# Dividing the softmax by its sum after the product with the values, with the reciprocals spread by two transposes a block

## The chip, the cores and the metric

One NeuronCore of a Trainium2 chip. The metric is the device time of one execution in microseconds (us). Engines are named as in the profile: PE (TensorE), PEld (its weight load), DVE (VectorE), ACT (ScalarE), POOL (GpSimd), SP (the queue that issues DMAs).

## What is computed

For 4 images of 8 heads (768 rows, 64 columns a head) the reference hashes q and k with 6 projections, lets a row see only the keys with its own hash, and takes an exact softmax:

```python
scores = scale * np.matmul(q, k.transpose(0, 1, 3, 2))
scores = np.where(mask, scores, -1000000000.0)
scores = scores - np.max(scores, axis=-1, keepdims=True)
attn = np.exp(scores)
attn = attn / (np.sum(attn, axis=-1, keepdims=True) + 1e-09)
return np.matmul(attn, v).astype(np.float32)
```

The heads laid side by side (512 columns) then go through a gated feed-forward stage: `h = relu(x @ w_in)`, a 3-tap convolution along the rows, `h * sigmoid(conv) @ w_out`, 1024 hidden columns. The weights and taps arrive as 64-bit floats.

## The kernel before, in words

The four images are worked one after the other. An image has four pairs of heads; a pair has three **blocks** of 256 query rows; a block has four **units** (2 heads x 2 tiles of 128 rows). So there are 192 units and 48 blocks. `Pair.prepare` (L202 on) splits q and k of the next pair into high and low parts on POOL (L167, L172) and has SP copy them into place (L170, L174), and hashes on PE (L182); the hash bits pass DVE (L185) and POOL (L187).

A unit passes these steps:

- `products` (L249, PE): scores s, 4 matmuls into PSUM ring S, which has three slots for s, the transposes t and the hash;
- `maximum` (DVE): L257 copies s to SBUF tile e and takes the row maximum; `total` (L264) adds 1e-9 to the sum of the unit before; L261 scales the maximum;
- `exponential` (L267, ACT): exp, with the row sum gathered into column 2 of the small tile st;
- `normalise`, one unit later: reciprocal of the sum (L272, DVE), then e times it (L273, POOL, 128x768);
- `transposes` (L278, PE), LAG = 3 units later: six 128x128 transposes of e into ring S; `to_sbuf` (L285, ACT) copies them to at.

After the transposes of a block's last unit its `values` are listed: 6 chunks x 2 heads on PE (L298, 24 matmul instructions, here "the v group") into half of a 512-column PSUM tile of ring M (two slots). They run in one go in the next iteration of four (AVS = (6, 0, 0, 0)), behind that iteration's transposes. An iteration later ACT copies the result to xh (L303), and one more later DVE puts the rest in xl (L306): x is kept as a high and a low part. For the last block of an image the values run inside the feed-forward stage (`fill`, L461), after its first `hidden`.

The loop (L408 on) writes out the order of each engine by hand; engines run in order and wait for one another by semaphores. In an iteration come: products, maximum, transposes and copy of unit i-3, exp, normalise of unit i-1, xl, the v group, a step of `prepare`, then `background`. `background` (L125) runs the decoding of weights from 64-bit floats: 16 blocks of 128x512, each with five DVE steps (L87, L89, L91, L93, L95), ACT casts (L85, L103) and two POOL steps (L105, L107), one block begun every 3.6 iterations. It lasts through the first image and into its feed-forward stage. `ffn` (L367) has hidden matmuls (L323), activation and taps (L328 to L342) and the output matmuls (L353).

Of the kernel before, what the change touches and what calls it, by code (L numbers as in the profile page):

```python
# [7 lines left out]
F32 = mybir.dt.float32  # L8
# [4 lines left out]
ALU = mybir.AluOpType  # L13

B, H, S, D = 4, 8, 768, 64
NB = 6
DM, DFF = 512, 1024
P = 128
NP = H // 2
NCK = S // P  # L20
HS = S // 2
QB = 256
# [6 lines left out]
F64_MIN = 2.0 ** -15 * 1.125  # L29
LAG, EB = 3, 5  # L30
FLAG = 3
AVS = (6, 0, 0, 0)
PREP = (3, 2, 1)
PREP_N = 6
W0 = 6
# [6 lines left out]
def lsh_attention_conv_ffn(ctx, tc, qk, v, hw, w_in, conv_w, w_out, consts, ident_in, out):  # L42
    nc = tc.nc
    PSUM = bass.MemoryType.PSUM
    cp = ctx.enter_context(tc.tile_pool(name="const", bufs=1))
    wp = ctx.enter_context(tc.tile_pool(name="work", bufs=1))
# [4 lines left out]
    def ring(pool, bufs, shape, dtype, tag, name):  # L51

        k = turns[tag] = (turns.get(tag, -1) + 1) % bufs
        return pool.tile(shape, dtype, tag=f"{tag}{k}", name=name, bufs=1)


    ident = cp.tile([P, P], F32, name="ident")
# [51 lines left out]
    def decode_taps(raw):  # L109
        up, low = yield from decode(raw, NFC * 3, "cw")  # L110
        nc.vector.tensor_tensor(cw.rearrange("p f k -> p (f k)"), up, low, ALU.add)
# [7 lines left out]
    def fetch(n):  # L119

        for src, name in blocks[:n]:
            raw = cp.tile([P, 2 * WC], I32, tag=f"w{name}", name=f"raw{name}")
            nc.sync.dma_start(raw, src)
            fetched.append((raw, name))
        del blocks[:n]  # L125
# [111 lines left out]
    class Unit:  # L237
# [11 lines left out]
                    nc.tensor.matmul(self.sp[:, half, :HS], A[:, h, qs], C[:, h, half * HS:(half + 1) * HS],  # L249
                                     start=(kk == 0), stop=(kk == 1))  # L250

        def maximum(self, prev):

            self.st = ring(wp, 8, [P, 4], F32, "st", f"st{self.nm}")
            e = wp.tile([P, 776], F32, tag="e", name=f"e{self.nm}", bufs=EB)
            self.e = e[:, :S]
            nc.vector.tensor_scalar(self.e.rearrange("p (a b) -> p a b", a=2), self.sp[:, :, :HS],  # L257
                                    MASKED, None, ALU.max, ALU.max, accum_out=self.st[:, 0:1])
            if prev:
                prev.total()  # L260
            nc.vector.tensor_scalar(self.st[:, 1:2], self.st[:, 0:1], -SCALE, None, ALU.mult)  # L261

        def total(self):
            nc.vector.tensor_scalar(self.st[:, 2:3], self.st[:, 2:3], 1e-9, None, ALU.add)  # L264

        def exponential(self):
            nc.scalar.activation(self.e, self.e, AF.Exp, bias=self.st[:, 1:2], scale=SCALE,  # L267
                                 accum_out=self.st[:, 2:3])

        def normalise(self):  # L270
            st = self.st
            nc.vector.reciprocal(st[:, 3:4], st[:, 2:3])  # L272
            nc.gpsimd.tensor_scalar(self.e, self.e, st[:, 3:4], 0.0, ALU.mult, ALU.add)  # L273

        def transposes(self):
            self.tp = ring(ps, 3, [P, 2, 512], F32, "S", f"t{self.nm}")
# [8 lines left out]
            nc.scalar.copy(pr.at[self.h][:, :, :, self.tq * P:(self.tq + 1) * P],  # L285
                           self.tp[:, :, :3 * P].rearrange("p j (c q) -> p j c q", c=3))

    def values(pr, qb, ats):

        if qb == 0:  # L290
            pr.x = [ring(wp, NP, [P, S], F32R, f"x{k}", f"x{k}{pr.nm}")
                    for k in "hl"]
        vt, (xh, xl) = pr.v, pr.x
        av = ring(ps, 2, [P, 512], F32, "M", f"v{pr.nm}_{qb}")

        def chunk(c):
            for h in range(2):
                nc.tensor.matmul(av[h * D:(h + 1) * D, :QB], vt[:, c, h, :],  # L298
                                 ats[h][:, c // 3, c % 3, :],
                                 start=(c == 0), stop=(c == NCK - 1), tile_position=(0, h * D))  # L300

        def out_high():
            nc.scalar.copy(xh[:, cols], av[:, :QB])  # L303

        def out_low():
            nc.vector.tensor_tensor(xl[:, cols], av[:, :QB], xh[:, cols].bitcast(F32), ALU.subtract)  # L306

        cols = slice(qb * QB, (qb + 1) * QB)
        return [lambda c=c: chunk(c) for c in range(NCK)], (out_high, out_low)


    g2, prep = [None], [iter(())]
# [54 lines left out]
    def ffn(b, xs, fill, last):  # L367
# [4 lines left out]
        for i in range(len(todo) + FLAG):  # L372
# [17 lines left out]
            if i < len(todo):  # L390
# [5 lines left out]
    units = [Unit(pr, t, h) for pr in pairs for qb in range(S // QB) for h in range(2)  # L396
             for t in range(qb * QB // P, (qb + 1) * QB // P)]
# [8 lines left out]
    av, outs, lows, early = [], [], [], None  # L406
    n = len(units)
    for i in range(n + LAG):  # L408
        u = units[i] if i < n else None
        before = units[i - 1] if 1 <= i <= n else None  # L410
        w = units[i - LAG] if i >= LAG else None
        pi, k = divmod(i, 2 * NCK)
        done, outs, lows = lows, [], outs
        for high, low in lows:
            high()
        ending = w and w.pair.p == NP - 1 and w.qb == S // QB - 1
        if u:
            u.products()
        if ending:
            for high, low in done + lows:  # L420
                low()
            done, lows = [], []
        if u:
            u.maximum(before)
        elif before:
            before.total()
        if w and w is not early:
            w.transposes()
            w.to_sbuf()
        if u:  # L430
            u.exponential()
        if i in (0, 2):
            next(first, None)
        if before:
            before.normalise()
        for high, low in done:
            low()
        for _ in range(NCK if ending else AVS[(i - LAG) % 4]):
            if av:
                steps, last = av[0]  # L440
                steps.pop(0)()
                if not steps:
                    outs.append(last)
                    av.pop(0)
        if u and k == PREP[min(pi, 2)] and pi + 1 < len(pairs):
            prep[0] = pairs[pi + 1].prepare()
        next(prep[0], None)
        if u and k == PREP[min(pi, 2)] + PREP_N and pi + 1 < len(pairs):
            pairs[pi + 1].load_v()
            if pi + 2 < len(pairs):  # L450
                pairs[pi + 2].load()
        if i == 3:
            splits.append(decode_taps(cwr))
        if i >= W0 - 4:
            fetch(i % 3 == 0)
        if i >= 1:
            background(RATE if i >= W0 else 0, 1)
        if w and w.tq == QB // P - 1 and w.h == 1:
            if not ending:
                av.append(values(w.pair, w.qb, w.pair.at))  # L460
            else:  # L461
                def fill():
                    steps, last = values(w.pair, w.qb, w.pair.at)
                    for step in [*steps, *last]:
                        step()

                bi = w.pair.b
                early = units[i + 1 - LAG] if i + 1 - LAG < n else None

                def transposes_ahead():  # L470
                    if early:
                        early.transposes()
                        early.to_sbuf()
                        turns["S"] -= 1

                ffn(bi, [pairs[bi * NP + c].x for c in range(NCC)], fill, transposes_ahead)
# [43 lines left out]
```

## Time and profile before

| what | value |
|---|---|
| median of 3 runs (769.47, 774.13, 773.67) | 773.67 us |
| the profiled execution: its time, its span | 770.6 us, 768.8 us |
| mean granted TensorE clock | 0.981 |
| busy in the span: PE, DVE, ACT, POOL | 723.8, 509.6, 510.4, 399.9 us |
| first image: attention, feed-forward | 0 to 157, 157 to 250 us |
| images 1 to 3 | 250 to 769 us |

Busy shares are means over stages with different limits. A matmul's record overlaps with those of its neighbours, so PE's pace is read from the starts of instructions, or from the chain of waits, not from the mean duration.

### The profile page before, as it was taken

To read this page: it belongs to the slowest core of one execution; us is meant where nothing else is said; L and a number is where in the kernel's file an instruction comes from. 1 tells how busy PE (TensorE), PEld (TensorE's weight loads), DVE (VectorE), ACT (ScalarE), POOL (GpSimd) and SP (SyncE) were. 2 spreads that over 40 slices of the span, in tenths; PEclk is the share of its full clock that TensorE was granted. 3 is DMA by queue.
4 is the path that set the end of the run, shared out by engine and by line. 5 is a ranking of instruction groups with operands and counts; after the bars stand their busy time and mean duration, and the time that the engine had idled before them with its cause. 6 is when DMAs were issued, how large, how long until landed. Compare 5 with 4: busy or idle time off the path is not lost.

```text
span 768.8 us, 13591 instructions
## 1 busy us (share of the span) xinstructions
PE 723.8 (94%) x4552; PEld 585.8 (76%) x4552; DVE 509.6 (66%) x1320; ACT 510.4 (66%) x954; POOL 399.9 (52%) x373
## 2 busy tenths in 40 slices
PE   6977878998899999999999999999999999999997
PEld 3755556677788777778998777778998787778986
DVE  8858789988875556665665665565755666654653
ACT  5756677774456777786555887776555877875553
POOL 4747788864563556553522466653622475532322
PEclk9979999998999999999999999999999999999999
DMA  3665564820033164452312064652211154400011
GB/s 110 156 192 134 168 167 142 216 88 1 0 106 121 24 165 117 128 148 51 82 42 83 21 152 115 161 152 51 67 56 40 65 125 118 105 1 1 1 42 41
DMA packets 30357, 72.18 MB, mean 94 GB/s; under 512 B 5936, under 2 KB 7504, under 8 KB 30288
## 3 DMA queue, kind: packets, MB, share of 16 engines
q1 hardware_dynamic: 30000, 71.27, 33.8%
q8 instruction: 36, 0.59, 0.3%
q14 instruction: 33, 0.27, 0.1%
q10 hardware_dynamic: 288, 0.05, 0.0%
HBM read 27.40 MB, written 6.29 MB: 44 GB/s over the span
## 4 chain that ended last, share of the span: by engine, by line
PE 75%; DVE 12%; DMA 4%; issue 3%; ACT 2%; POOL 2%; SPq 1%; DVEq 0%; POOLq 0%
PE o L353 15%; PE v L298 15%; PE h L323 15%; PE s L249 14%; PE t L278 13%; DVE e L257 4%; DMA R<-in_qk 2%; DVE ht L332 2%; DMA k<-R 2%; PE hash L182 1%; POOL e L273 1%; SPq L170 1%; DVE wuo L87 1%; ACT e L267 1%; DVE wlo L93 0%
## 5 line engine op out<-in xcount | busy, mean ns | idle before, releaser
L273 POOL TENSOR_SCALAR e<-e,st 128x768 f32<-128x768 f32 x192 | 180.5, 940 | 183.0 <-ACT at L285 92.1
L257 DVE TENSOR_SCALAR_CACHE_REDUCE e<-s 128x768 f32<-128x768 f32 x192 | 183.3, 955 | 108.5 <-PE s L249 101.0
L267 ACT ACTIVATE e<-e,st 128x768 f32<-128x768 f32 x192 | 181.0, 943 | 33.5 <-DVE st L272 28.2
L285 ACT COPY at<-t 128x768 f32<-128x768 f32 x192 | 152.2, 793 | 63.9 <-PE t L278 63.7
L278 PE MATMUL t<-ident,e 128*128 128x128 f32 x1152 | 164.3, 280 | 19.2 <-DVE st L264 16.8
L278 PEld LDWEIGHTS t<-ident,e 128*128 128x128 f32 x1152 | 131.2, 143 | 46.6 <-POOL e L273 21.4
L342 POOL TENSOR_TENSOR g<-ht,g 128x384 fp32r<-128x384 f32 x64 | 73.0, 1140 | 170.1 <-ACT g L341 144.6
L332 DVE SCALAR_TENSOR_TENSOR ht<-ht,cw 128x384 f32<-128x384 f32 (+1 forms) x128 | 116.1, 907 | 65.0 <-ACT ht L330 62.7
L323 PE MATMUL h<-xh,wi 128*128 128x386 f32 x512 | 144.2, 345 | 5.3 <-ACT ht L328 5.1
L353 PE MATMUL o<-wo,g 128*128 128x512 f32 x576 | 144.7, 398 | 2.5 <-ACT osb L359 1.3
L298 PE MATMUL v<-at,v 128*64 128x256 f32 x1152 | 138.4, 389 | 0.1
L353 PEld LDWEIGHTS o<-wo,g 128*128 128x128 f32 x576 | 108.1, 190 | 24.5 <-ACT osb L359 1.7
L249 PE MATMUL s<-K,Q 128*128 128x384 f32 x384 | 118.2, 390 | 4.7 <-DVE e L257 2.1
L298 PEld LDWEIGHTS v<-at,v 128*64 128x64 f32 x1152 | 81.5, 139 | 44.2 <-issue 10.9
L323 PEld LDWEIGHTS h<-xh,wi 128*128 128x128 f32 x512 | 95.4, 190 | 10.9 <-ACT ht L328 7.5
L249 PE MATMUL s<-k,q 96*128 96x384 f32 x384 | 101.2, 345 | 1.9 <-DVE e L257 1.8
L335 ACT ACTIVATE ht<-ht 128x384 f32<-128x384 f32 x64 | 33.7, 526 | 93.2 <-DVE ht L332 93.2
L323 PE MATMUL h<-xl,wi 128*128 128x386 f32 x256 | 87.9, 343 | 0.0
L249 PEld LDWEIGHTS s<-K,Q 128*128 128x128 f32 x384 | 59.6, 195 | 35.9 <-issue 19.0
L249 PEld LDWEIGHTS s<-k,q 96*128 96x128 f32 x384 | 72.0, 194 | 3.2 <-ACT q L229 2.9
L336 DVE TENSOR_TENSOR ht<-ht 128x384 f32<-128x384 f32 x64 | 43.2, 675 | 31.7 <-ACT ht L335 31.7
L172 POOL TENSOR_TENSOR R<-R,hi 128x768 fp32r<-128x768 f32 x30 | 58.1, 1936 | 0.0
(66 smaller groups left out, 593.2 us busy)
## 6 DMA issues: line engine op xcount, KB each, us to landing
R<-in_qk SPq DMA_DIRECT2D x15, 768.0 KB
K<-hi SPq DMA_DIRECT2D x60, 192.0 KB
v<-in_v SPq DMA_DIRECT2D x16, 384.0 KB
out<-osb SPq DMA_DIRECT2D x24, 256.0 KB
Q<-hi SPq DMA_DIRECT2D x30, 192.0 KB
q<-hi SPq DMA_DIRECT2D x30, 192.0 KB
Q<-R SPq DMA_DIRECT2D x30, 192.0 KB
k<-R SPq DMA_DIRECT2D x30, 192.0 KB
```

Of the source, the lines that this page charges most:

```text
L172: nc.gpsimd.tensor_tensor(lo, R, hi.bitcast(F32), ALU.subtract)
L249: nc.tensor.matmul(self.sp[:, half, :HS], A[:, h, qs], C[:, h, half * HS:(half + 1) * HS], start=(kk == 0), stop=(kk == 1))
L257: nc.vector.tensor_scalar(self.e.rearrange("p (a b) -> p a b", a=2), self.sp[:, :, :HS], MASKED, None, ALU.max, ALU.max, accum_out=self.st ...
L267: nc.scalar.activation(self.e, self.e, AF.Exp, bias=self.st[:, 1:2], scale=SCALE, accum_out=self.st[:, 2:3])
L273: nc.gpsimd.tensor_scalar(self.e, self.e, st[:, 3:4], 0.0, ALU.mult, ALU.add)
L278: nc.tensor.transpose(self.tp[:, c // 3, c % 3 * P:(c % 3 + 1) * P], self.e[:, c * P:(c + 1) * P], ident)
L285: nc.scalar.copy(pr.at[self.h][:, :, :, self.tq * P:(self.tq + 1) * P], self.tp[:, :, :3 * P].rearrange("p j (c q) -> p j c q", c=3))
L298: nc.tensor.matmul(av[h * D:(h + 1) * D, :QB], vt[:, c, h, :], ats[h][:, c // 3, c % 3, :], start=(c == 0), stop=(c == NCK - 1), tile_posi ...
L323: nc.tensor.matmul(hp[:, :HW], w, x[:, c0:c0 + HW], start=(n == 0), stop=(n == 3 * NCC - 1))
L332: nc.vector.scalar_tensor_tensor(t[:, a:z], ht[:, o + k - 1 + a:o + k - 1 + z], cw[:, f, k:k + 1], t[:, a:z], ALU.mult, ALU.add)
L342: nc.gpsimd.tensor_tensor(g[:, 1, :], t, g[:, 0, :].bitcast(F32), ALU.subtract)
L353: nc.tensor.matmul(op, l, r, start=(f == 0 and n == 0), stop=(f == NFC - 1 and n == 2))
```

## The change

The exponentials are no longer divided: they are transposed and multiplied with the values as they are, and the product is divided. `total` and `normalise` go for all 192 units. The exp's row sums are gathered into one tile `sums` a block (128 x 2 x 2). Two iterations after a block's last unit, `reciprocals` adds 1e-9 to the four columns, takes four reciprocals (DVE), and POOL writes each 64 times over into `rec` (128 x 256). Ahead of the v group two transposes on PE bring `rec` into the other half of the PSUM tile of the product, so that it lies over the product's layout (heads over partitions, rows along the columns). ACT copies that to `rs` (in the place of its copy to xh), DVE multiplies product and rs into x (in the place of xl), and POOL makes xh and xl of x. A scratch area of the DMA system is made smaller, for room.

```diff
-AVS = (6, 0, 0, 0)
+AVS = (1 + NCK, 0, 0, 0)
...
-            if prev:
-                prev.total()
...
-        def total(self):
-            nc.vector.tensor_scalar(self.st[:, 2:3], self.st[:, 2:3], 1e-9, None, ALU.add)
...
-                                 accum_out=self.st[:, 2:3])
-
-        def normalise(self):
-            st = self.st
-            nc.vector.reciprocal(st[:, 3:4], st[:, 2:3])
-            nc.gpsimd.tensor_scalar(self.e, self.e, st[:, 3:4], 0.0, ALU.mult, ALU.add)
+                                 accum_out=self.sums[:, self.tq, self.h:self.h + 1])
+
+        def reciprocals(self):
+
+            nc.vector.tensor_scalar(self.sums, self.sums, 1e-9, None, ALU.add)
+            nc.vector.reciprocal(self.sums, self.sums)
+            pr = self.pair
+            pr.rec = ring(wp, 1, [P, QB // P, 2, D], F32, "rec", f"rec{self.nm}")
+            nc.gpsimd.tensor_scalar(pr.rec, self.sums.unsqueeze(3).to_broadcast([P, QB // P, 2, D]), 1.0, 0.0,
+                                    ALU.mult, ALU.add)
...
+        def spread():
+
+            for t in range(QB // P):
+                nc.tensor.transpose(av[:, QB + t * P:QB + (t + 1) * P],
+                                    rec[:, t].rearrange("p h d -> p (h d)"), ident)
+
...
-        def out_high():
-            nc.scalar.copy(xh[:, cols], av[:, :QB])
-
-        def out_low():
-            nc.vector.tensor_tensor(xl[:, cols], av[:, :QB], xh[:, cols].bitcast(F32), ALU.subtract)
-
+        def factors():
+            nc.scalar.copy(rs, av[:, QB:2 * QB])
+
+        def out():
+            x = ring(wp, 2, [P, QB], F32, "x32", f"x{pr.nm}_{qb}")
+            nc.vector.tensor_tensor(x, av[:, :QB], rs, ALU.mult)
+            nc.gpsimd.tensor_scalar(xh[:, cols], x, 1.0, 0.0, ALU.mult, ALU.add)
+            nc.gpsimd.tensor_tensor(xl[:, cols], x, xh[:, cols].bitcast(F32), ALU.subtract)
+
+        rs = ring(wp, 2, [P, QB], F32, "rs", f"rs{pr.nm}_{qb}")
         cols = slice(qb * QB, (qb + 1) * QB)
-        return [lambda c=c: chunk(c) for c in range(NCK)], (out_high, out_low)
+        return [spread, *(lambda c=c: chunk(c) for c in range(NCK))], (factors, out)
...
+        two = units[i - 2] if 2 <= i <= n + 1 else None
+        if two and two.tq == QB // P - 1 and two.h == 1:
+            two.reciprocals()
...
-        if before:
-            before.normalise()
...
-    nc = bacc.Bacc("TRN2", target_bir_lowering=False, num_devices=1)
+    nc = bacc.Bacc("TRN2", target_bir_lowering=False, num_devices=1, dynamic_dma_scratch_size=1024)
```

## Rows read from the trace of the kernel before

**Rows 1.** Engine time by stage (columns: stretch, its length, busy by engine, PE clock, DMA).

```profile
25.00:157.00 132.00, 108.06 (x723) 79.84 (x723) 109.92 (x290) 89.18 (x164) 98.44 (x82) 0.92 0.61 171
...
419.00:519.00 100.00, 99.69 (x743) 77.18 (x742) 62.77 (x245) 78.64 (x147) 57.98 (x61) 1.00 0.49 130
```

**Rows 2.** Chain of waits, 450 to 480 us (start, length, what).

```profile
459.37 0.84 PE t L278 x6
460.21 2.74 PE v L298 x24
...
469.71 2.74 PE v L298 x24
...
478.34 1.66 PE v L298 x14
```

**Rows 3.** Waits, 25 to 157 us, PE (us in total, times, longest).

```profile
PE t L278 <- DVE st L264: 16.8, 12, 3.0
...
PE hash L182 <- DMA R<-in_qk: 2.0, 1, 2.0
```

**Rows 4.** Engine time of single blocks, from v group to v group.

```profile
55.68:69.18 13.50, 10.31 (x67) 7.64 (x65) 11.05 (x26) 7.58 (x14) 10.15 (x8) 0.87 0.35 89
...
141.50:151.60 10.10, 9.07 (x65) 6.74 (x65) 8.78 (x27) 7.81 (x14) 9.70 (x8) 1.00 0.79 183
433.37:442.88 9.51, 9.51 (x73) 7.03 (x72) 5.92 (x23) 7.48 (x14) 4.58 (x6) 1.00 0.01 3
```

**Rows 5.** Timeline of one long stop of PE in the first image.

```profile
74.65 1.44 POOL L105 TENSOR_TENSOR wui<-wui,wi 128x512 f32<-128x512 f32 x1
75.01 1.63 DVE L91 SCALAR_TENSOR_TENSOR wui<-wui,wli 128x512 int32<-128x512 int32 x1
76.07 1.34 POOL L273 TENSOR_SCALAR e<-e,st 128x768 f32<-128x768 f32 x1
...
77.66 1.52 PE L278 MATMUL t<-ident,e 128*128 128x128 f32 x6 [2.97 <-DVE st L264]
```

**Rows 6.** Timeline of PEld and POOL at the last image's end.

```profile
690.85 1.29 PEld L278 LDWEIGHTS t<-ident,e 128*128 128x128 f32 x12 [0.39 <-issue]
693.23 0.64 PEld L278 LDWEIGHTS t<-ident,e 128*128 128x128 f32 x6 [1.09 <-POOL e L273]
```

**Rows 7.** Timeline of DVE around two maxima, 40 us.

```profile
40.12 0.14 DVE L264 TENSOR_SCALAR st<-st 128x1 f32<-128x1 f32 x1
40.23 0.15 DVE L261 TENSOR_SCALAR st<-st 128x1 f32<-128x1 f32 x1
40.30 0.16 DVE L272 RECIPROCAL st<-st 128x1 f32<-128x1 f32 x1
40.38 0.69 DVE L87 SCALAR_TENSOR_TENSOR wui<-wli,rawi 128x512 f32<-128x512 f32 x1
```

**Rows 8.** Timeline of DVE, 48 to 53 us, with POOL idle.

```profile
50.11 0.42 DVE L93 TENSOR_SCALAR wli<-wui 128x512 int32<-128x512 int32 x1
50.56 0.69 DVE L95 SCALAR_TENSOR_TENSOR wli<-rawi,wli 128x512 f32<-128x512 uint32 x1
```

**Rows 9.** Groups by line, 48 to 157 us (busy, mean ns of one | idle before).

```profile
L172 POOL TENSOR_TENSOR R<-R,hi 128x768 fp32r<-128x768 f32 x6 | 12.3, 2047 | 0.0
...
L91 DVE SCALAR_TENSOR_TENSOR wui<-wui,wli 128x512 int32<-128x512 int32 x6 | 8.4, 1396 | 0.2
L95 DVE SCALAR_TENSOR_TENSOR wli<-rawi,wli 128x512 f32<-128x512 uint32 x7 | 8.2, 1168 | 0.2
...
L89 DVE TENSOR_SCALAR wli<-wui 128x512 int32<-128x512 int32 x6 | 4.8, 808 | 0.0
```

**Rows 10.** Groups by line, whole span.

```profile
L273 POOL TENSOR_SCALAR e<-e,st 128x768 f32<-128x768 f32 x192 | 180.5, 940 | 183.0 <-ACT at L285 92.1 <-DVE st L272 79.3 <-PE s L249 4.0
...
L278 PE MATMUL t<-ident,e 128*128 128x128 f32 x1152 | 164.3, 280 | 19.2 <-DVE st L264 16.8 <-POOL e L273 2.3
...
L306 DVE TENSOR_TENSOR xl<-v,xh 128x256 fp32r<-128x256 f32 x48 | 19.6, 408 | 7.4 <-ACT xh L303 7.4
```

More of the change, by code (lines that the diff above doesn't have):

```diff
@@ L250, in products, with maximum @@
                                      start=(kk == 0), stop=(kk == 1))
-        def maximum(self, prev):
-            self.st = ring(wp, 8, [P, 4], F32, "st", f"st{self.nm}")
+        def maximum(self):
+            self.st = ring(wp, 8, [P, 2], F32, "st", f"st{self.nm}")
+            if self.tq == 0 and self.h == 0:
+                self.pair.sums = ring(wp, 3, [P, QB // P, 2], F32, "sums", f"sums{self.nm}")
+            self.sums = self.pair.sums
             e = wp.tile([P, 776], F32, tag="e", name=f"e{self.nm}", bufs=EB)
@@ L286, in to_sbuf, with values @@
                            self.tp[:, :, :3 * P].rearrange("p j (c q) -> p j c q", c=3))
-    def values(pr, qb, ats):
+    def values(pr, qb, ats, rec):
         if qb == 0:
@@ L409, in lsh_attention_conv_ffn @@
         u = units[i] if i < n else None
-        before = units[i - 1] if 1 <= i <= n else None
         w = units[i - LAG] if i >= LAG else None
@@ L423, in lsh_attention_conv_ffn @@
         if u:
-            u.maximum(before)
-        elif before:
-            before.total()
+            u.maximum()
+        two = units[i - 2] if 2 <= i <= n + 1 else None
+        if two and two.tq == QB // P - 1 and two.h == 1:
+            two.reciprocals()
         if w and w is not early:
@@ L433, in lsh_attention_conv_ffn @@
             next(first, None)
-        if before:
-            before.normalise()
         for high, low in done:
             low()
-        for _ in range(NCK if ending else AVS[(i - LAG) % 4]):
+        for _ in range(1 + NCK if ending else AVS[(i - LAG) % 4]):
             if av:
@@ L459, in lsh_attention_conv_ffn @@
             if not ending:
-                av.append(values(w.pair, w.qb, w.pair.at))
+                av.append(values(w.pair, w.qb, w.pair.at, w.pair.rec))
             else:
                 def fill():
-                    steps, last = values(w.pair, w.qb, w.pair.at)
+                    steps, last = values(w.pair, w.qb, w.pair.at, w.pair.rec)
                     for step in [*steps, *last]:
```

## The prediction

> **What bounds the kernel now.** I read the page's busy shares first: PE 94%, DVE and ACT 66%, POOL 52%. Means hide stages, so next come the engine times by stage. In the later images' attention PE is busy 99.69 of 100 us, and every other engine has a fifth or more to spare [rows 1]. In the first image's attention (25 to 157 us) PE has 108 of 132 us, DVE 110, POOL 98, at a mean clock of 0.92 [rows 1]. These are two regimes, and the change is priced in each.
>
> In the later images the chain of waits runs on PE alone: scores, transposes, v group. From v group to v group a block takes 478.34 - 469.71 = 8.63 us, or 469.71 - 460.21 = 9.50 us with a hash [rows 2]. Only what PE issues counts there; what DVE, ACT or POOL save is slack.
>
> In the first image a block takes 10.1 to 13.5 us, and the same block in a later image 9.5 with a hash [rows 4] or 8.63 without [rows 2]. The eight blocks from 55.68 to 151.60 take 95.9 us; at the later pace (two have a hash) they would take 6 x 8.63 + 2 x 9.50 = 70.8. The excess is 25.1 us: all that the change can win there. The waits say why: PE's transposes waited 16.8 us in 12 waits for DVE [rows 3]. The ring of scores has three slots, so a unit's transposes need the slot of the scores before, and these are released by their maximum on DVE. DVE has weight decoding between two maxima; the timeline shows a stop of 2.97 us so made, and the transposes behind it take 1.52 us [rows 5], as the clock has dropped: the block has a mean clock of 0.87 [rows 4], at the lower level of 1.2 GHz for part of it. Three of the eight blocks have 0.87.
>
> **The change part by part.**
>
> *Two transposes a block on PE* (added). Twelve transposes in a row load in 1.29 us, and six in 0.64 [rows 6]: 0.11 us each. A block adds 0.22 us. They stand behind transposes of the same shape, ahead of the v group, so the switch to the v group is paid as before. In images 1 to 3 nothing hides them: 36 x 0.22 = +7.9 us. In the first image PE is late half of the time; I charge them all, 12 x 0.22 = +2.6 (between 0 and 2.6).
>
> The Trainium skill ("TensorE: Matmul & The Clock Gate", Part 4: PE-mode transpose) gives one 128x128 transpose about 390 ns alone and about 275 ns in a kernel. The mean record of a transpose here, 280 ns [rows 10], looks the same, but records overlap, and the pace is 0.11 us [rows 6]; by the page's 275 ns the two would add 48 x 0.55 = 26 us, an estimate from that page.
>
> *`total` and `normalise`' reciprocal on DVE* (removed). Of four steps from 40.12 to 40.38 [rows 7] two go. The three small operations take 0.26 us in a row; one alone should take about 0.09 (the starts lie 0.07 to 0.11 apart), so 0.17 us a unit is won. A block adds two operations on four columns, some 0.2 us. One unit in four lies beside the v group, where DVE has time. Per block 3 x 0.17 - 0.2 = 0.31; eight blocks give -2.5 us (0 to -3.5). In later images: nothing, since PE covers it.
>
> *The normalise on POOL* (removed, 192 x 0.94 us [rows 10]). In the later images POOL had slack: 0. In the first its worth is indirect. Weight steps on DVE that take 0.69 and 0.42 us with POOL idle [rows 8] take 1.40, 1.17 (L91, L95) and 0.81 (L89) on the average [rows 9]; in the long stop L91 takes 1.63 beside L105 and then L273 [rows 5]. So POOL beside them costs 0.71 + 0.48 + 0.39 = 1.58 us a weight block, and with one weight block begun every 3.6 units, some nine fall into the 32 units of these eight blocks: 14 us. Not all goes: L105, L107 and L172 stay on POOL, and rec, xh and xl come in, right behind the reciprocals and the product, where weight steps follow. I take half, 7 us, and three units in four on the path: -5.3 us (0 to -10.7).
>
> *The clock.* Where the two stops of nearly 3 us shrink (the second is the one shown), the half-speed stretch behind each goes too: the six transposes take 1.52 [rows 5] instead of 6 x 0.11 = 0.66, and I let the v group behind them lose nearly as much, an estimate. About 1.6 us each, two of the three: -3.2 (0 to -4.8).
>
> *Products with the reciprocals.* DVE's xl (0.41 us [rows 10]) becomes a multiplication of the same size and place, also with one PSUM input: 0. ACT copies the same number of elements: 0; it no longer waits for the end of the v group, since the factors come ahead of it. POOL gets rec, xh and xl. No row shows them at this width. For rec and xh (256 columns) a third of L273 is 0.31, all of it 0.94; I take 0.45. For xl half of L105 [rows 5] is 0.72, all of it 1.44; I take 0.75. That is 1.65 us a block, against 3.76 removed. All of it beside PE; xh and xl are wanted by the hidden matmuls a unit later at the earliest, and the last pair's come last in each sum.
>
> *New waits.* The spread waits for rec, and behind it on PE stand the v group and all else. The reciprocals are issued two iterations ahead, some 3 us at the later pace. In the later images POOL is idle by then: 0. In the first, L172 (2.05 us [rows 9]) or L105 and L107 may stand ahead: 0 to 2 us a block; I take 0, as POOL has lost more than it got. DVE's multiplication waits for ACT's copy of the factors, ready earlier than xh was; behind it stand weight steps and the next maximum. POOL's xh waits for DVE, and behind it stands the split of the next pair, whose DMAs SP issues; they come earlier on the average, as L273 is no longer ahead of them. One hash waited 2.0 us for such a load [rows 3]; that chain is DMA, and I take 0 (0 to -2).
>
> *The end.* The last unit's transposes wait 1.09 us for POOL's normalise [rows 6], of which the matmuls before cover about 0.2: -0.9. The exp, which they need now, is done by then. The scratch size: 0.
>
> **Sum.** First image: +2.6 - 2.5 - 5.3 - 3.2 = -8.4. Later images +7.9, the end -0.9. Together -1.4 us: 769.2 against the profiled execution's 770.6. That execution lies 3.1 us below the median of the runs, 773.67, so on their scale it is 772.3 us. What a measurement can tell from no change is about 1%, here 7.7 us.
>
> **The rivals.**
>
> A. *The first image comes near PE's pace.* For it: POOL's normalise starts right behind the reciprocal, just when DVE starts its weight step, so the collision was systematic, and the new POOL work is less than half. Against: three decoding steps a weight block remain between the maxima, 1.1 us in a unit, even without collision. If four fifths of the 25.1 us go, -20.1 + 2.6 + 7.9 - 0.9 = -10.5: 763.2 us.
>
> B. *POOL, no longer held back, runs into DVE and into PE elsewhere.* The normalise paced POOL to DVE. Without it L105 and L107 start as soon as ACT has cast, and L172 behind the bits: the weight steps collide as often, and rec stands behind L172 and L105. Its price: L172 2.05 and L105 1.44 and rec 0.45 are 3.9 us against 3 us of lead, and L107, of L105's size, makes it 5.4: 0.9 to 2.4 us a wait, with the clock drop of 1.6 behind the longer ones. With no saving but the small operations (-2.5) and waits of 2 us in a third of twelve blocks (+8): +2.6 - 2.5 + 8 + 7.9 - 0.9 = +15.1, 789 us. If the collisions stay, it decides from a single such wait on: +7.1 without one. For it: POOL is 75% busy in that stage [rows 1]. Against: it has 2.1 us less to do a block.
>
> C. *A transpose costs its record, not its pace*, by draining PE ahead of the v group: 2 x 0.28 x 48 = 26.9 instead of 10.5, with all else as forecast: +15.0, 789 us. The Trainium skill's figure (same section) would make this one. Against: twelve in a row keep 0.11 [rows 6].
>
> D. *The division does not leave the path.* Not possible for L273: its line goes. But L261 and the maxima, which hold PE, stay; that is inside the forecast.
>
> **How the numbers follow.** Forecast 0.59, with its own range 765 to 780; A 0.22; B 0.15; C 0.04. Faster by over 1% (under 766): A, 0.22. Slower by over 1% (over 781.4): B and C, 0.19. Within: 0.59. For 8 in 10 the range goes to the middle of A and into B's lower half: 762 to 784.
>
> **What the profile would show.** Right: later blocks of about 8.85 and 9.72 us from v group to v group, PE still without gaps; L91 and L95 nearer 0.9 than 1.3; no stop near 3 us at the first image's transposes; blocks there between 10 and 12 us; POOL's busy time down by some 100 us (180 less, 80 more). Wrong: v groups or spreads that wait for POOL's rec; weight steps as slow as before, now beside L105, L107 or L172; a block of later images longer by more than 0.3 us.

## The result, and the profile after

Over 13 runs each the changed kernel takes 766.76 us (median) and the kernel before 772.04: a ratio of 0.9937 (95% interval 0.9917 to 0.9958), 4.9 us less. Within 1%, as forecast, and inside the range; but the sum came out by terms that were not all right. The first of the changed kernel's 13 executions took 1005.5 us at a mean granted clock of 0.655; it is out of the ratio, and the profile shown is that of a later execution (the first run below, 763.9 us of span against 768.8).

From the page of the changed kernel, engine time over the span:

```profile
PE 723.5 (95%) x4648; PEld 593.3 (78%) x4648; DVE 489.5 (64%) x1032; ACT 510.1 (67%) x954; POOL 296.0 (39%) x325
```

POOL lost 104 us of work, DVE 20; PE has as much as before, in 4.9 us less. Where the time went is read by stages. The first image's feed-forward stage begins with the first hidden matmul. In the timeline of PE, kernel before:

```profile
157.41 0.42 PE L323 MATMUL h<-xh,wi 128*128 128x386 f32 x1
```

and changed kernel:

```profile
144.87 0.42 PE L334 MATMUL h<-xh,wi 128*128 128x386 f32 x1
```

The first image's attention is 12.5 us shorter. The stretches behind it, engine times of the kernel before (first image's feed-forward stage, then all to the last output matmul):

```profile
157.41:241.47 84.06, 76.28 (x370) 65.50 (x369) 63.17 (x79) 44.77 (x88) 45.02 (x34) 0.96 0.15 40
241.47:764.61 523.14, 520.60 (x3375) 427.86 (x3373) 314.99 (x903) 359.27 (x678) 242.14 (x240) 1.00 0.30 81
```

and of the changed kernel:

```profile
144.87:230.64 85.77, 76.27 (x372) 65.53 (x371) 64.83 (x77) 44.71 (x87) 44.75 (x35) 0.96 0.15 39
230.64:759.61 528.97, 526.80 (x3447) 438.00 (x3445) 300.75 (x691) 359.17 (x678) 169.00 (x206) 1.00 0.30 80
```

So -12.5 in the first image's attention, +1.7 in its feed-forward stage, +5.8 in the other three images: -5.0, which is the difference of the spans within rounding.

Not all of the 12.5 us lie in the eight blocks that the prediction works from. Engine times of the block ahead of them and of these eight, from start to start of their v groups, kernel before:

```profile
34.25:52.28 18.03, 13.05 (x73) 9.00 (x72) 13.63 (x36) 8.89 (x17) 9.63 (x9) 0.75 0.85 238
52.28:148.83 96.55, 78.34 (x530) 58.77 (x529) 80.49 (x210) 66.53 (x121) 77.22 (x63) 0.94 0.58 157
```

and changed kernel:

```profile
34.83:48.26 13.43, 10.86 (x76) 8.12 (x75) 11.87 (x24) 8.60 (x18) 7.41 (x9) 0.92 0.81 243
48.26:135.26 87.00, 75.61 (x546) 57.62 (x545) 75.58 (x165) 66.03 (x121) 57.19 (x55) 0.99 0.67 173
```

The eight blocks start 4.0 us earlier, take 9.5 us less, and 1.0 us is lost behind them. What comes earlier ahead of them is the split of the next pair on POOL and the loads behind it. POOL and SP in the timeline, kernel before:

```profile
19.90 0.83 POOL L167 TENSOR_SCALAR hi<-R 128x768 fp32r<-128x768 f32 x1
43.68 0.39 SPq L154 DMA_DIRECT2D R<-in_qk  x1
```

and changed kernel:

```profile
17.63 1.06 POOL L167 TENSOR_SCALAR hi<-R 128x768 fp32r<-128x768 f32 x1 [3.43 <-DMA R<-in_qk]
40.40 0.39 SPq L154 DMA_DIRECT2D R<-in_qk  x1
```

(L167 begins the split, two passes of POOL stood ahead of it; L154 loads the pair after.) In the block ahead of the eight, PE waits in the kernel before 1.9 us for a copy of the split (Q<-R) and 2.0 for this load; in the changed kernel 2.6 for the load alone.

In images 1 to 3 the chain of waits of the changed kernel answers to [rows 2]:

```profile
461.73 0.22 PE v L300 x2
461.94 2.74 PE v L305 x24
...
468.45 0.41 DVE x L314
468.85 0.88 DVE e L259 x2
...
469.78 0.87 PE t L279 x6
470.66 0.22 PE v L300 x2
470.87 2.74 PE v L305 x24
```

The two transposes (L300) take 0.22 us, as worked out. A block without a hash takes 470.87 - 461.94 = 8.93 us instead of 8.63; one with a hash took 9.57 to 9.60 instead of 9.50 (starts of v groups in PE's timeline), not 9.72. But the chain is no longer PE's alone: between the maxima of a block's second and third unit (an expectation below counts them from the v group, as third and fourth) it runs over DVE's multiplication (L314), and the transposes ahead of the v group come late. PE's weight load shows this stop in the timeline:

```profile
469.78 0.64 PEld L279 LDWEIGHTS t<-ident,e 128*128 128x128 f32 x6 [0.38 <-DVE e L259]
```

In the first image's attention, 25 to 145 us, engine times of the kernel before:

```profile
25.00:145.00 120.00, 97.51 (x649) 72.63 (x648) 98.89 (x259) 79.08 (x146) 89.95 (x75) 0.91 0.61 166
```

and of the changed kernel:

```profile
25.00:145.00 120.00, 103.89 (x749) 78.73 (x748) 103.46 (x226) 89.53 (x165) 71.91 (x72) 0.99 0.68 183
```

In the same 120 us PE issues 749 matmul instructions instead of 649, and the mean clock is 0.99 instead of 0.91. Of PE's waits in that stretch (changed kernel) the first is the one of [rows 3], 11.1 us instead of 16.0 in the same stretch (16.8 up to 157), the longest 1.5 instead of 3.0:

```profile
PE t L279 <- DVE e L259: 11.1, 13, 1.5
```

The weight steps, groups by line from 48 to 157 us, changed kernel (answering to [rows 9]; "wui" and "wli" are blocks of w_in, "wuo" blocks of w_out):

```profile
L87 DVE SCALAR_TENSOR_TENSOR wui<-wli,rawi 128x512 f32<-128x512 f32 x6 | 6.7, 1110 | 2.0 <-ACT wli L85 2.0
L91 DVE SCALAR_TENSOR_TENSOR wuo<-wuo,wlo 128x512 int32<-128x512 int32 x4 | 6.7, 1680 | 0.1
L95 DVE SCALAR_TENSOR_TENSOR wli<-rawi,wli 128x512 f32<-128x512 uint32 x7 | 6.3, 899 | 0.2
L91 DVE SCALAR_TENSOR_TENSOR wui<-wui,wli 128x512 int32<-128x512 int32 x6 | 5.2, 872 | 0.2
```

and kernel before, the group that [rows 9] leaves out:

```profile
L91 DVE SCALAR_TENSOR_TENSOR wuo<-wuo,wlo 128x512 int32<-128x512 int32 x3 | 4.2, 1398 | 0.1
```

In the blocks of w_in L91, L95 and L89 fell by 0.52, 0.27 and 0.12 us (L89 to 0.68), and L87 rose from 0.77 to 1.11: in the timeline L105, L107, L167 or L172 lie beside its longest. In the blocks of w_out L91 rose, from 1.40 to 1.68. Over all steps of both kinds in the first image's attention a weight block takes 4.53 us of DVE instead of 4.83.

### The profile page after: what moved, and what is told of

It is laid out like the page before. It is cut to its first block, busy times and chain, and to the rows that moved or that the text cites. A ratio compares the mean times of both kernels' runs of the same rounds, so it can differ in the third digit from the quotient of the medians.

```text
span 1002.8 us, 12954 instructions
## 1 busy us (share of the span) xinstructions
PE 991.0 (99%) x4648; PEld 695.6 (69%) x4648; DVE 493.1 (49%) x1032; ACT 523.0 (52%) x954; POOL 294.1 (29%) x325
## 4 chain that ended last, share of the span: by engine, by line
PE 97%; DVE 2%; DMA 0%; issue 0%
PE v L305 19%; PE h L334 19%; PE o L364 19%; PE s L249 18%; PE t L279 18%; PE hash L182 2%; PE v L300 1%; DVE e L259 1%; DMA hw_sb<-in_hw 0%; DVE wui L91 0%; PE hash L210 0%; DVE wli L89 0%; DVE wli L95 0%; DVE x L314 0%; DVE k L225 0%
## 5 line engine op out<-in xcount | busy, mean ns | idle before, releaser
L279 PE MATMUL t<-ident,e 128*128 128x128 f32 x1152 | 223.1, 346 | 0.6 <-DVE e L259 0.3
L364 PE MATMUL o<-wo,g 128*128 128x512 f32 x576 | 198.2, 507 | 0.0
L279 PEld LDWEIGHTS t<-ident,e 128*128 128x128 f32 x1152 | 169.2, 159 | 40.3 <-DVE e L259 2.6
L305 PE MATMUL v<-at,v 128*64 128x256 f32 x1152 | 196.0, 509 | 0.0
L334 PE MATMUL h<-xh,wi 128*128 128x386 f32 x512 | 183.9, 429 | 0.0
L249 PE MATMUL s<-K,Q 128*128 128x384 f32 x384 | 146.6, 466 | 0.8 <-POOL K L216 0.7
L273 POOL TENSOR_SCALAR rec<-sums 128x256 f32<-128x256 f32 x48 | 19.4, 405 | 388.8 <-DVE sums L270 369.3
L249 PE MATMUL s<-k,q 96*128 96x384 f32 x384 | 126.6, 416 | 2.1 <-DVE e L259 2.1
L334 PE MATMUL h<-xl,wi 128*128 128x386 f32 x256 | 109.5, 428 | 0.0
L339 ACT ACTIVATE ht<-h 128x386 f32<-128x386 f32 x64 | 31.2, 488 | 94.4 <-PE h L334 94.4
```

The source lines that it names most:

```text
L279: nc.tensor.transpose(self.tp[:, c // 3, c % 3 * P:(c % 3 + 1) * P], self.e[:, c * P:(c + 1) * P], ident)
L334: nc.tensor.matmul(hp[:, :HW], w, x[:, c0:c0 + HW], start=(n == 0), stop=(n == 3 * NCC - 1))
L339: nc.scalar.activation(ht[:, :HW], hp[:, :HW], AF.Relu)
L364: nc.tensor.matmul(op, l, r, start=(f == 0 and n == 0), stop=(f == NFC - 1 and n == 2))
```

## The experiments

"First stage" below is the start of the first image's feed-forward stage (157.4 before, 144.9 changed); "a block" is a block without a hash in images 1 to 3, from v group to v group.

### The changed kernel again

> The changed kernel as it is, for a profile at the full clock. By the forecast's steps: 765 to 770 us; from v group to v group 8.85 us (9.72 with a hash) in images 1 to 3, against 8.63 and 9.50 before; the eight blocks of the first image that took 95.9 us take 85 to 89; no stop of PE near 3 us there and no block with a mean clock under 0.95; L91 and L95 nearer 0.9 than 1.3 us. Rival (POOL runs into DVE elsewhere): L91 and L95 stay at 1.2 to 1.4 us, and PE's transposes or the spread wait for POOL.

766.38 us, ratio to the kernel before 0.9949 (0.9930 to 0.9968). It is the profile shown above. The total is as expected; a block is 8.93, not 8.85; the eight blocks named took 87.0 us (v groups at 48.26 to 135.26; from start to start they took 96.6 before), with none of the stops near 3 us left. One of the eight ran at a mean clock under 0.95 (0.94).

### Without the two transposes

```diff
         def spread():
-            for t in range(QB // P):
-                nc.tensor.transpose(...)
+            pass
...
-            nc.scalar.copy(rs, av[:, QB:2 * QB])
+            nc.scalar.copy(rs, rec.rearrange("p t h d -> p (t h d)"))
```

> The changed kernel without the two transposes a block; ACT copies the reciprocals as they stand in SBUF, so that the product is multiplied by numbers that are not spread over the partitions. Theory (the transposes cost PE's pace, nothing hides them in images 1 to 3): 48 x 0.22 = 10.5 us less than the changed kernel, at least 7.9; 755 to 759 us. Rival (they cost their record of 0.28 us each): 25 us less, 742. Rival (they fill a stop ahead of the v group that is there anyway): 0 to 3 us less.

758.72 us, 7.7 less than the changed kernel beside it: the transposes cost their pace, in images 1 to 3. The first stage starts at 145.14 us, no earlier than with them (144.87), so this profile shows no price in the first image. Its eight blocks took 85.7 us against 87.0, but began 1.4 us later, at 49.68, where profiles of the same first image scatter (47.6 to 49.3); a price of about a microsecond is not excluded. Chain of waits:

```profile
458.54 2.74 PE v L303 x24
467.21 2.74 PE v L303 x24
475.90 2.74 PE v L303 x24
```

A block is 8.67 to 8.69 us. Without the transposes the changed kernel should have been faster here than the kernel before (8.63), which has POOL's pass and two more small operations on DVE a unit. It is slower; that is the place of DVE's work, below.

### Without POOL's pass

```diff
             nc.vector.reciprocal(st[:, 3:4], st[:, 2:3])
-            nc.gpsimd.tensor_scalar(self.e, self.e, st[:, 3:4], 0.0, ALU.mult, ALU.add)
```

> The kernel before without the multiplication on POOL (L273); the reciprocals on DVE stay, the softmax is not divided. Theory (POOL's pass slows the weight steps on DVE beside it): 5.3 + 3.2 + 0.9 = 9.4 us less than before, all of it in the first image and at the end: 762 to 765 us, with the weight steps L91 and L95 near 0.9 us. Rival (the collisions only move to L105, L107 and L172): within 2 us of before, weight steps as slow as before. Rival (a transposes' wait for the pass itself is what counts): less than before, but with L91 and L95 unchanged.

754.12 us, 0.9788 (0.9767 to 0.9809): 16.1 us less, more than the 9.4 expected. First stage at 144.53 us: POOL's pass alone makes the whole gain of the first image up to there, with the small operations still in. In images 1 to 3 a block is a little shorter too (chain of waits):

```profile
454.35 2.74 PE v L297 x24
462.91 2.74 PE v L297 x24
471.49 2.74 PE v L297 x24
```

8.56 to 8.58 us. L91 took 1.26 us, L95 0.77, L89 0.67 and L87 1.13 in the stretch of [rows 9]: L91 did not come near 0.9, and the sum of the four fell from 4.14 to 3.84, so the weight steps are only part of it. The mean clock from 25 to 145 us is 0.99.

### The changed kernel with POOL's pass kept

```diff
+        def hold(self):
+            nc.gpsimd.tensor_scalar(self.e, self.e, 1.0, 0.0, ALU.mult, ALU.add)
...
+        if 1 <= i <= n:
+            units[i - 1].hold()
         for high, low in done:
             low()
```

> The changed kernel with a pass of POOL over e kept at the old place (times one, waiting for the exp, not for a reciprocal). Theory: the gain in the first image is POOL's pass, so this one pays the transposes and loses that gain: 9.4 us more than the changed kernel, 774 to 778 us, slower than before. Rival (the small operations on DVE are the gain): within 2 us of the changed kernel.

786.89 us, 1.0218 (1.0192 to 1.0243): 20.5 us more than the changed kernel, twice what was expected. First stage at 158.74 us, so the gain of the first image is gone. The rest is new: with the pass and rec, xh and xl together POOL is late in the other images, where a block takes 9.07 to 9.1 us: from 243 us on PE's weight load waits 13.3 us, in 24 waits, for the pass.

### POOL's pass beside, read by nobody

```diff
+    sink = cp.tile([P, S], F32, name="sink")
...
+        def beside(self):
+            nc.gpsimd.tensor_scalar(sink, self.e, 1.0, 0.0, ALU.mult, ALU.add)
```

(called where the pass was kept above)

> The changed kernel with a pass of POOL over each e, like the removed one in size and place in POOL's order, but written to a tile that nobody reads: POOL and the ports to SBUF are loaded as before, and no transpose waits for it. Theory 1 (the pass costs as load: it slows DVE's weight steps, and POOL's later steps come late): as slow as the run that kept the pass, 783 to 789 us, first image's attention over 155 us. Theory 2 (the transposes' wait for the pass is the cost): within 3 us of the changed kernel, 764 to 769 us, first image's attention 145 to 148 us.

781.29 us, 1.0116 (1.0088 to 1.0143), a little under the range expected; first stage at 157.72 us, as before the change. No wait of PE or its weight load is for this pass, and DVE waits 1.8 us for it in the whole span; yet all 12.5 us are back. So the wait for its result is not what it costs. What is left is that it runs at all, beside DVE, and that it stands in POOL's order, where it waits for the exp and holds up what comes behind it; this run keeps both and does not part them. In the stretch of [rows 9] the weight steps (one line further down here) are slow again, L95 with 1.19 us and L91 with 1.18, and the mean clock from 25 to 145 us is 0.91:

```profile
L92 DVE SCALAR_TENSOR_TENSOR wui<-wui,wli 128x512 int32<-128x512 int32 x6 | 7.1, 1184 | 0.2
```

A block is 8.90 us, as in the changed kernel, with some longer ones in image 2.

### A narrow pass

```diff
-            nc.gpsimd.tensor_scalar(self.e, self.e, st[:, 3:4], 0.0, ALU.mult, ALU.add)
+            nc.gpsimd.tensor_scalar(self.e[:, ::6], self.e[:, ::6], st[:, 3:4], 0.0, ALU.mult, ALU.add)
```

> The kernel before with POOL's multiplication on every sixth column alone (128 columns instead of 768), so that the wait of the transposes and the reciprocals stay and the load goes; the softmax is divided in those columns only. Theory 1 (load): near the run without the pass, 754 to 758 us. Theory 2 (wait): near the kernel before, over 766 us.

768.82 us, 0.9957 (0.9935 to 0.9979), first stage at 153.79. By its total it lies in the range of the second theory, the wait (over 766), by the first image between the two. The group of the pass says why the first theory was not put to the test as meant:

```profile
L273 POOL TENSOR_SCALAR e<-e,st 128x128 f32<-128x128 f32 x192 | 104.8, 546 | 254.4 <-ACT at L285 117.0 <-DVE st L272 112.9 <-PE hash L182 9.3
```

With a sixth of the columns, taken at a stride, the pass still took 0.55 us instead of 0.94. More than half of the load stayed. The run tells something else. The weight steps became nearly as short as without any pass (their sum up to the first stage is 48.8 us, against 48.0 without it and 54.7 before), and still only 3.6 us were won there: the length of the weight steps is not the main cost of the pass. And the load of R that the changed kernel issues at 40.40 us came at 43.57, as before; without the pass it comes at 40.42. The split of the next pair began at 19.8 us, as before, behind two passes: there it is the pass's place in POOL's order that costs, not its length.

### Reciprocals and product ahead of the first maximum

```diff
+        if 1 <= i <= n and units[i - 1].tq == QB // P - 1 and units[i - 1].h == 1:
+            units[i - 1].reciprocals()
...
-        if ending:
+        if True:
             for high, low in done + lows:
                 low()
...
-        two = units[i - 2] if 2 <= i <= n + 1 else None
-        if two and two.tq == QB // P - 1 and two.h == 1:
-            two.reciprocals()
```

> The changed kernel with two places moved: the reciprocals one iteration earlier and the multiplication of the product two earlier, both ahead of the maximum, where DVE has nothing to do beside the v group. Theory (in images 1 to 3 a block lost 0.30 us, 0.22 to the two transposes and 0.08 to DVE's sums, reciprocals and product between the maxima of the third and fourth unit): a block without a hash goes from 8.92 to about 8.79 us, 24 such blocks give 2 to 3 us; with a little of the first image 761 to 764.5 us. Rival (the multiplication waits for the copy of the factors, and holds the first maximum behind the v group): 766 us or more.

772.66 us, 1.0007 (0.9994 to 1.0020): slower than the changed kernel, in the rival's range, and still the theory of the later images held, by more than expected. Chain of waits there:

```profile
470.15 2.74 PE v L305 x24
...
478.80 2.74 PE v L305 x24
```

8.65 us a block with both transposes in, 0.28 less than with the late place. The loss is elsewhere. In the first image ACT is late, as the rival had it, and the multiplication holds the maximum behind it (timeline of DVE; 8.1 us in 6 waits from 25 to 145 us):

```profile
65.39 0.42 DVE L314 TENSOR_TENSOR x<-v,rs 128x256 f32<-128x256 f32 x1 [1.03 <-ACT rs L310]
65.73 0.95 DVE L259 TENSOR_SCALAR_CACHE_REDUCE e<-s 128x768 f32<-128x768 f32 x1
```

First stage at 155.18 us. And behind each feed-forward stage no v group covers the reciprocals' wait for the exp; PE stops for 1.66 us (timeline of PE):

```profile
421.19 0.87 PE L279 MATMUL t<-ident,e 128*128 128x128 f32 x6 [1.66 <-DVE e L259]
```

### The changed way in the first image alone

The code of both kernels side by side; what chooses is:

```diff
+            self.late = self.pair.b == 0
...
-        if two and two.tq == QB // P - 1 and two.h == 1:
+        if two and two.late and two.tq == QB // P - 1 and two.h == 1:
...
+        if before and not before.late:
+            before.normalise()
```

> The changed way in the first image alone, the way before in images 1 to 3. Theory (the gain lies in the first image, 12.5 us up to its feed-forward stage, and the later images only pay for the two transposes and DVE's place): faster than both, 756 to 760 us; from v group to v group 8.63 us in images 1 to 3. Rival (the later images gain too, at the ends of their stages): 764 us or more.

759.72 us, 0.9847 (0.9820 to 0.9875): faster than both. First stage at 144.76 us, a block 8.63. The gain of the change lies in the first image; the rest was its cost.

### No pass and no small operations

```diff
-            if prev:
-                prev.total()
...
-            nc.vector.reciprocal(st[:, 3:4], st[:, 2:3])
-            nc.gpsimd.tensor_scalar(self.e, self.e, st[:, 3:4], 0.0, ALU.mult, ALU.add)
+            pass
```

> The kernel before without POOL's multiplication and without the two small operations of each unit on DVE (the sum's 1e-9 and the reciprocal); the softmax is not divided. Against the run without POOL's pass alone this prices the small operations. Forecast: 2.5 to 3.5 us less in the first image, nothing in the later ones. Theory now (they lie between two maxima, and these hold the transposes): 0.1 to 0.2 us a block in images 1 to 3 as well, 8.57 to 8.4 us, so 5 to 8 us less in all: 746 to 750 us. Rival (PE covers them): 752 to 755 us.

752.15 us, 0.9745 (0.9702 to 0.9788); the run without the pass alone had 0.9788 (0.9767 to 0.9809), and the total lies in the range of the rival, that PE covers them; the intervals overlap, so the totals do not part the two. The chain of waits does:

```profile
457.01 2.74 PE v L295 x24
465.45 2.79 PE v L295 x24
473.94 2.78 PE v L295 x24
```

8.44 and 8.49 us, against 8.57: the small operations cost about 0.1 us a block in images 1 to 3, where I had put nothing. In the profile the first stage began at 148.06 us, later than without the pass alone (144.53), at a mean clock of 0.94 against 0.99 from 25 to 145 us; the first image does not show their worth.

### Two places

```diff
+            self.ahead = pair.b > 0 and (pair.p, self.qb) != (0, 0)
...
+        if one and one.tq == QB // P - 1 and one.h == 1 and one.ahead:
+            one.reciprocals()
...
-        if ending:
+        if ending or (w and w.pair.b > 0):
```

> The changed way in all images. In the first image the reciprocals and the multiplication of the product stand where the change has them; in images 1 to 3 they stand ahead of the first maximum, beside the v group, save the reciprocals of each image's first block, for which no v group gives cover. Theory (both places were measured: 144.9 us up to the first feed-forward stage with the late one, 8.65 us a block with the early one, and the early one's stop of 1.65 us behind a feed-forward stage goes): 757 to 760 us, as fast as the run with the old way in the later images, with the two transposes in. Rival (the gain of the early place in images 1 to 3 came from something else than the place): 763 us or more.

759.79 us, 0.9858 (0.9827 to 0.9890), first stage at 144.82 us, and the chain of waits in image 2:

```profile
458.90 2.74 PE v L306 x24
467.32 0.22 PE v L301 x2
467.54 2.74 PE v L306 x24
...
476.19 2.74 PE v L306 x24
```

8.64 and 8.65 us. Both halves of the theory hold: the changed way costs no more than the old one in the later images if DVE's work stands beside the v group.

### The first image alone, and one small operation less

```diff
-            if prev and not prev.late:
-                prev.total()
```

> The run with the changed way in the first image alone, and in images 1 to 3 without the operation that adds 1e-9 to a row's sum; the sum has at least one term that is exactly 1, so the addition changes nothing in 32 bits, and what is left out is only that. Theory (each small operation between two maxima costs): 8.55 us a block, 2 to 4 us less than with it, 755 to 758 us. Rival (PE covers it): 758.5 to 761 us.

757.05 us, 0.9822 (0.9787 to 0.9857). Chain of waits:

```profile
462.24 2.74 PE v L311 x24
470.76 2.74 PE v L311 x24
479.30 2.74 PE v L311 x24
```

8.52 and 8.54 us a block, 0.1 less than with the addition: this is shown. The total is the lowest median of a kernel with the whole computation save that addition, but its interval overlaps with those of the two runs above. Its profiled execution began the first stage at 149.6 us, at a clock of 0.94, though its first image runs the same code as that of the run with the changed way there alone (144.76).

### The kernel before again

> The kernel before once more, for a second profile: how far does its first image scatter? If the 12.5 us between the profiles (157.4 against 144.9 us up to the first feed-forward stage) are the change's, this one starts that stage at 154 to 160 us, with a mean clock of 0.92 to 0.95 in the first image's attention and stops of PE near 3 us; if they are scatter, below 150. From v group to v group 8.63 us either way.

A single time of 770.03 us. First stage at 157.75, and the same row as above:

```profile
25.00:145.00 120.00, 97.41 (x649) 72.50 (x648) 98.70 (x256) 78.83 (x145) 89.83 (x74) 0.91 0.60 165
```

So two profiles of the kernel before agree within 0.4 us, and four with the changed first image (the changed kernel, the one without the transposes, the changed way in the first image alone, the two places) lie at 144.8 to 145.1. The 12.5 us are the change's, with the one profile at 149.6 as a mark of the scatter. What the clock has to do with that one shows in the eight blocks: the code of the first image is the same in the run with the changed way there alone,

```profile
47.55:135.20 87.65, 76.25 (x545) 58.32 (x544) 76.13 (x166) 66.22 (x121) 57.96 (x57) 0.98 0.68 175
```

and in the run with one small operation less,

```profile
49.31:140.07 90.76, 79.50 (x546) 60.21 (x545) 74.51 (x164) 66.13 (x121) 56.13 (x55) 0.94 0.62 167
```

PE is idle for 11.4 and 11.3 us; the 3.1 us between them are all in its busy time, at a clock of 0.94 instead of 0.98.

## Why the prediction came out

**The total, in part by luck.** Forecast -1.4 us, measured -4.9. First image's attention: -8.4 forecast, -12.5 found. Images 1 to 3 with the end: +7.0 forecast, +5.8 found (+6.7 against the second profile of the kernel before). The first image's feed-forward stage: 0 forecast, +1.7 found, which hid part of the gain that was missed. That is not scatter: from the start of its first matmul to that of its last the stage took 85.1 to 85.5 us in the five profiles with the changed first image, and 83.5 to 83.7 in the two of the kernel before and the two without the pass; its cause was not looked for. In images 1 to 3 two errors cancelled: a block without a hash rose by 0.30 us, not 0.22, and one with a hash by 0.08.

**The first image, in its parts.** The forecast was worked out for the eight blocks, with "all that the change can win there": -8.4 against the -9.5 found, which is near. PE's idle time in them fell by 6.8 us and its busy time by 2.7. What it left out lies ahead of them: 4.0 us. What failed there is the term "that chain is DMA, and I take 0 (0 to -2)": the split of the next pair stands behind the pass in POOL's order; without it the split starts at 17.6 instead of 19.9 us, the load behind it is issued at 40.4 instead of 43.7, PE waits 1.3 us less for DMAs at a clock of 0.92 instead of 0.75, and the third v group starts at 48.26 instead of 52.28. With the narrow pass next to none of this came (load at 43.57, v group at 52.00), with the unread pass a third (41.76 and 50.84), without the pass all of it (40.42 and 47.86).

**Two transposes a block.** Right in price (0.22 us, in the chain of waits) and in images 1 to 3 (7.7 us less without them, 7.9 forecast). In the first image, where +2.6 was charged, the run without them shows no later start of the first stage that they would account for; about 1 us is not excluded. Rival C, a transpose at its record of 0.28 us, is out. The Trainium skill ("TensorE: Matmul & The Clock Gate", Part 4: PE-mode transpose) gives about 275 ns for one in a kernel (its 390 ns alone are for bf16, and these are f32); that is the length of the record here (276 to 280 ns), and the chain goes on after 0.22 us for two.

**POOL's pass.** That it pays to drop the pass, though POOL has slack, was right: unread, it puts the 12.5 us back. The way in which it pays is shown only in part. Weight steps on DVE up to the first stage, all 57 of both kinds, summed from the traces:

| run | weight steps, us | first stage at |
|---|---|---|
| kernel before | 54.7 | 157.4 |
| changed kernel | 51.5 | 144.9 |
| without POOL's pass | 48.0 | 144.5 |
| pass beside, read by nobody | 54.7 | 157.7 |
| narrow pass | 48.8 | 153.8 |

I summed L91, L95 and L89 to a saving of 0.79 us a weight block, half of the collisions. In the blocks of w_in these three gave 0.91, and L87 gave back 0.34; over both kinds a block gained 0.30, for L105, L107 and L172 now lie beside the steps, the part of rival B that came true. So this term (-5.3) was too large, and the narrow pass, with the steps shortened and little won, says the same. In images 1 to 3 "POOL had slack: 0" was off by 0.06 us a block, and by 0.14 for one with a hash.

**The clock.** I took -3.2 us, for two stops. It was right in kind and somewhat small. At a mean of 0.91 from 25 to 145 us, some 22 us ran at 1.2 GHz, at 0.99 some 2; but 9 of the 22 lie in the block ahead of the eight (mean 0.75), in which PE waited 3.9 us for DMAs and 1.0 for a maximum. The eight blocks went from 0.94 to 0.99. Two profiles of one code took 3.1 us more at 0.94 than at 0.98, so I put the clock at some 4 us of the 9.5, an estimate from these two.

**`total` and `normalise`' reciprocal.** The -2.5 us in the first image no run shows: without them as well the first stage came later, at a lower clock. "In later images: nothing, since PE covers it" failed. PE was busy 99.7% there, and still one operation less a unit took 0.1 us off a block. The sign stood in [rows 2]: the six transposes ahead of the v group take 0.84 us of the chain, where the first six of a block take 0.66. PE's weight load is idle for 0.28 us ahead of them; the records of matmuls overlap, and PE's busy time hides it. Without the pass they still take 0.81, without the small operations as well 0.68, and in the run with two places (chain of waits, image 2)

```profile
466.66 0.66 PE t L280 x6
```

**Products with the reciprocals: 0.** Failed, by 0.28 us a block without a hash (with one, 9.58 us in either place). Sums, reciprocals and product stand in one place between two maxima, and the transposes ahead of the v group wait. Moving them ahead of the first maximum took the 0.28 back. I priced the operations by size and saw that xl had the same one; I did not ask where the three stand together. These failures partly cancel: the small operations and the pass gone (some 0.2) and the new place (0.28) make up for one another but for some 0.1 us, and the transposes' 0.22 is left. Nor is ACT's copy of the factors free of the v group (timeline of ACT, changed kernel):

```profile
464.73 0.37 ACT L310 COPY rs<-v 128x256 f32<-128x256 f32 x1 [1.00 <-PE v L305]
```

It waits for the group, though the factors lie in the other half of the tile and were there before it; "it no longer waits for the end of the v group" failed. Whether the chip or the program's semaphores ask for this wait, no run tells. Between the v groups of images 1 to 3 nobody waits for the copy in the late place; at the end of each of their attentions, where the multiplication stands ahead of a maximum, DVE waits 3.2 us for it.

**New waits.** 0 was right: no spread waited for rec in the waits of PE or its weight load. Rival A did not come: from the third v group on, blocks of the first image still take 9.6 to 12.1 us. Rival B's price came only where the pass was kept beside the new work.

**The end.** Right: the last unit's stop of 0.9 us is gone (the last two v groups of the span lie 7.19 us apart instead of 8.08).

What stays open: how the 9.5 us of the eight blocks divide between the weight steps, POOL's order and the clock, as each shortens the others; and why some executions hold a clock of 0.94 there with the same code.

## What to carry to other kernels

Removing work from an engine with slack can pay where that engine shares time with one on the path: ask which of the path's operations run slower beside it, and what stands behind it in its own order, and test it with the same work done for nobody. A group of a profile that leaves out half of the same steps under another name can show a saving that the whole does not. Before adding work to an engine that is "covered", look where in its order it stands: the same three operations cost 0.28 us a block between two maxima and nothing beside the v group of a later image, and the best place differed between two stages of one kernel. A change that wins in one stage and pays in another can be used in the first alone.

## What the runs showed that was not expected

- A stage with PE at 99.7% of busy time was shortened from 8.63 to 8.44 to 8.49 us a block by work taken from DVE and POOL alone.
- A pass on POOL whose result nobody reads cost 12.5 us in a stage where POOL, without it, was idle 40% of the time (71.9 of 120 us busy).
- A third of the first image's gain came before the blocks that the prediction looked at: the split of the next pair no longer stood behind the pass in POOL's order, and the load behind it was issued 3.3 us earlier.
- On POOL 128 columns at a stride of six took 0.55 us, 768 in a row 0.94.
- Two halves of a PSUM tile were not independent for the reader here: ACT waited for matmuls into the other half, 31.5 us in 38 waits. Whether the chip or the program makes it wait is open.
